# Two attention steps per round with each exponential beside one FFN group, and another order of query chunks

## The chip, the cores and the metric

The kernel runs on one NeuronCore of a Trainium2 chip. The metric is the device time of the program in microseconds (us), the median over its runs. A ratio compares the fast runs of one kernel with those of the kernel before in the same rounds, on the same chip, so it is not quite the ratio of the medians that are quoted beside it. The three later sessions ran on three chips; across sessions, compare ratios rather than medians. Profiles come from one execution each.

Engines: PE is TensorE's matmuls, PEld its weight loads, ACT is ScalarE, DVE is VectorE, POOL is GpSimd, SP is the engine that issues most transfers. The granted clock is the share of full speed at which TensorE was allowed to run; 1.00 is full speed, and 0.50 I call half clock. A tile is a buffer; PSUM is the memory that takes TensorE's products.

## The reference, cut to what matters

A causal attention with 8 batches, 8 heads, 576 tokens, 64 channels per head and 16 extra "beacon" keys that every query sees, followed by a gated feed-forward network (FFN, often called ReGLU) over the 4608 tokens of all batches:

```python
k_all = concat([beacon_k, k]); v_all = concat([beacon_v, v])
scores = where(causal, -1e9, q @ k_all.T / 8)
x = softmax(scores) @ v_all                       # (8, 8, 576, 64) -> x: (4608, 512)
out = (relu(x @ w_gate) * (x @ w_val)) @ w_out    # 512 -> 1536 -> 512
```

## The kernel before

Heads are worked on in pairs `p` (four pairs per batch). The queries of a batch are cut into three chunks: chunk 0 has 240 columns and one step (step 0), chunk 1 has 256 columns and two steps (1 and 2), chunk 2 has 80 columns and one step (step 3). I call chunks 0 and 1 long and chunk 2 short.

One step is: score matmuls (L262), exp on ScalarE (L270), masks on GpSimd (L273), then, one round later, the products of exp with the values and with ones (L293). After a chunk's last step VectorE takes the reciprocal of the row sums (L300) and multiplies it in (L302), which writes `xT`, the input of the FFN. I call these two operations the epilogue of the chunk.

FFN work comes in groups. An "up" group is 4 gate matmuls (L320), a ReLU on ScalarE (L323), 4 value matmuls (L326) and a multiply on VectorE (L328). A "down" group is 12 matmuls (L333) and a copy. Both use the same two PSUM buffers `f`. An FFN tile of 512 tokens has 12 up and 4 down groups.

```python
CHUNKS = ((0, 240, 0, 0), (240, 256, 1, 2), (496, 80, 3, 3))   # first column, columns, first and last step
...
psb = main.enter_context(tc.tile_pool(name="psb", bufs=4))       # e, the exponentials
s_ps = main.enter_context(tc.tile_pool(name="s_ps", bufs=2, space=bass.MemoryType.PSUM))
o_ps = main.enter_context(tc.tile_pool(name="o_ps", bufs=2, space=bass.MemoryType.PSUM))
f_ps = main.enter_context(tc.tile_pool(name="f_ps", bufs=2, space=bass.MemoryType.PSUM))
...
    def up(self, nf, c0, c1):
        ...
        g = f_ps.tile([P, M_TILE], FP32, name="f")
        for ki in range(KM):
            nc.tensor.matmul(g[:, :n], wg[:, ki, nf * P:(nf + 1) * P], x[:, ki], ...)      # L320
        gs = fsb.tile([P, M_TILE], FP32, name="g")
        nc.scalar.activation(gs[:, :n], g[:, :n], AF.Relu)                                 # L323
        u = f_ps.tile([P, M_TILE], FP32, name="f")
        for ki in range(KM):
            nc.tensor.matmul(u[:, :n], wv[:, ki, nf * P:(nf + 1) * P], x[:, ki], ...)      # L326
        nc.vector.tensor_mul(self.h[:, nf, c0:c1], gs[:, :n], u[:, :n])                    # L328
...
# the main loop: a round ("double step") takes two attention steps and up to two FFN groups
for s0 in range(0, len(work) + STRIDE, STRIDE):
    ...
    for s in range(s0, s0 + STRIDE):
        for act in later.pop(s, []):     # loads, casts and transposes for the next batch
            act()
        if s < len(work):
            b, p, i = work[s]
            qk(pr, i)
            softmax(pr, i)
    for g in queue[:STRIDE]:             # two FFN groups
        g()
    del queue[:STRIDE]
    for s in range(s0 - STRIDE, s0):     # value products of the round before
        ...
        av(pairs[b, p], i)
```

In each batch `work` goes through chunk 0 of the four pairs, then chunk 1, then chunk 2. The scheduler is in manual mode, so each engine runs its instructions in the order in which they are written. 32 groups (the last two FFN tiles) are left over after the loop: the tail. After 4 of those groups stands a count that checks that all row sums are in range.

## Time and profile before

| | before |
|---|---|
| median of the first two runs | 486.41 us (485.93 to 486.9) |
| profiled span | 482.4 us |
| one batch in the steady part (119.27 to 165.95) | 46.68 us, 8 double steps |
| rounds of that batch with two up groups | 5.0, 6.2, 6.3, 5.4, 5.4, 5.2 us |
| start of batch 2 / the last round with scores | 119.27 / 392.79 us |

The page of the kernel before, its first lines and two rows of the timeline in 40 slices (each digit is the busy share in tenths):

```profile
span 482.4 us, 9099 instructions
PE 394.4 (82%) x3505; PEld 204.2 (42%) x3505; DVE 239.8 (50%) x322; ACT 190.3 (39%) x290; POOL 132.0 (27%) x293
PE   0113848777989998999899989998998899799994
DMA  9999997695569257824793396439720001002002
```

TensorE is nearly full from the eleventh slice (about 120 us) on. The first quarter is different: there the transfers are busy and TensorE is not. So two stages with different limits have to be read one by one.

The waits of the kernel before (engine, tile and line that waited, who it waited for, us in total, times, longest):

```profile
POOL half L238 <- DMA raw<-in_q_dram: 71.6, 25, 13.5
PE f L320 <- ACT g L323: 16.4, 33, 1.0
PE f L326 <- ACT g L323: 9.2, 14, 0.7
PE f L320 <- DVE xT L302: 7.1, 2, 6.9
```

In the steady part nearly all of TensorE's idle is a wait for the ReLU (`g`, L323). One round shows why. This is the timeline of the kernel before, from 177.51, first TensorE (start, duration, instruction, count, then the idle time before it and what ended it):

```profile
177.51 0.56 PE L262 MATMUL s<-qT,kT 64*128 64x256 bf16 x8
178.00 1.04 PE L320 MATMUL f<-xT,wg 128*128 128x512 bf16 x4
178.87 1.03 PE L326 MATMUL f<-xT,wv 128*128 128x512 bf16 x4
180.29 1.02 PE L320 MATMUL f<-xT,wg 128*128 128x512 bf16 x4 [0.39 <-ACT g L323]
182.00 1.02 PE L326 MATMUL f<-xT,wv 128*128 128x512 bf16 x4 [0.69 <-ACT g L323]
```

ScalarE and VectorE in the same round of the same timeline:

```profile
178.03 1.73 ACT L270 ACTIVATE e<-s 128x1024 bf16<-128x1024 f32 x2 [1.43 <-PE s L262]
179.64 0.60 ACT L323 ACTIVATE g<-f 128x512 f32<-128x512 f32 x1
181.35 0.60 ACT L323 ACTIVATE g<-f 128x512 f32<-128x512 f32 x1 [1.11 <-PE f L320]
...
177.90 1.65 DVE L300 RECIPROCAL r<-o 128x240 f32<-128x240 f32 x1
179.58 0.41 DVE L302 TENSOR_TENSOR xT<-o,r 128x240 bf16<-128x240 f32 x1
179.90 1.65 DVE L300 RECIPROCAL r<-o 128x240 f32<-128x240 f32 x1
181.58 0.41 DVE L302 TENSOR_TENSOR xT<-o,r 128x240 bf16<-128x240 f32 x1
181.91 0.68 DVE L328 TENSOR_TENSOR hT<-g,f 128x512 bf16<-128x512 f32 x1
```

The gate product is complete at about 179.0, but ScalarE is still in its second exponential and starts the ReLU at 179.64. The second gate product waits for the buffer that this ReLU frees. VectorE has two long epilogues in its queue (4.0 us), so the first FFN multiply comes only at 181.91. In the built program the second value product waits for ScalarE here: it was given the buffer of the second gate product, since the first value product's buffer is still held by that multiply (which reads it until 182.59, after the second value product has started). So it waits for the second ReLU, until 181.95.

### The profile page before, as it was taken

Reading aid. Unit: us, or ns where it says so; the run is one execution under the profiler, and the core shown is the slowest. Engines: PE = TensorE matmul, PEld = TensorE weight load, DVE = VectorE, ACT = ScalarE, POOL = GpSimd, SP = SyncE. Lnnn points to the kernel's source line nnn. Section 1 sums busy time; section 2 is a strip of 40 time slices with the busy share of each in tenths; the row PEclk is TensorE's granted clock in tenths of the full one; section 3 lists DMA queues with packets and bytes.
Section 4 is the critical chain, followed back from the end, with each engine's and each line's share of the span. In section 5 each row is a group of like instructions: output and inputs, shape, how many; then the busy total and the mean of one; then the engine's idle time right before and its main releaser. Section 6 shows DMA issues by size and latency. Waiting matters only on the chain.

```text
span 482.4 us, 9099 instructions
## 1 busy us (share of the span) xinstructions
PE 394.4 (82%) x3505; PEld 204.2 (42%) x3505; DVE 239.8 (50%) x322; ACT 190.3 (39%) x290; POOL 132.0 (27%) x293
## 2 busy tenths in 40 slices
PE   0113848777989998999899989998998899799994
PEld 0012635454434544454454445544454454244442
DVE  0033525855486448636762777277528653330320
ACT  2122414444445344534443445354444442122321
POOL 2162135343424332423251335134421110000000
PEclk9998859999999999999999999999999999899998
DMA  9999997695569257824793396439720001002002
GB/s 163 191 198 194 134 198 118 136 202 105 135 108 180 72 133 139 170 72 111 164 145 108 86 175 130 118 81 192 102 89 3 1 18 73 0 1 87 1 13 80
DMA packets 166145, 53.37 MB, mean 111 GB/s; under 512 B 155728, under 2 KB 161488, under 8 KB 166096
## 3 DMA queue, kind: packets, MB, share of 16 engines
q1 hardware_dynamic: 160320, 48.01, 49.2%
q0 software_dynamic: 5776, 4.72, 7.0%
q8 instruction: 29, 0.48, 0.4%
q14 instruction: 20, 0.16, 0.1%
HBM read 38.27 MB, written 9.44 MB: 99 GB/s over the span
## 4 chain that ended last, share of the span: by engine, by line
PE 52%; DMA 13%; SPq 9%; issue 8%; ACT 8%; DVE 5%; POOL 3%; ACTq 0%; DVEq 0%; POOLq 0%
PE f L333 19%; PE f L320 11%; PE f L326 11%; PE o L293 7%; DMA raw<-in_v_dram 6%; ACT g L323 5%; SPq L220 5%; DMA raw<-in_k_dram 5%; SPq L243 4%; DVE r L300 4%; PE s L262 3%; ACT e L270 3%; DMA raw<-in_q_dram 2%; POOL e L273 1%; POOL v L238 1%
## 5 line engine op out<-in xcount | busy, mean ns | idle before, releaser
L300 DVE RECIPROCAL r<-o 128x240 f32<-128x240 f32 (+2 forms) x96 | 129.9, 1353 | 91.4 <-PE o L293 76.3
L270 ACT ACTIVATE e<-s 128x736 bf16<-128x736 f32 (+3 forms) x128 | 103.7, 861 | 104.9 <-PE s L262 103.6
L320 PE MATMUL f<-xT,wg 128*128 128x512 bf16 (+2 forms) x480 | 116.2, 364 | 25.8 <-ACT g L323 16.4
L328 DVE TENSOR_TENSOR hT<-g,f 128x512 bf16<-128x512 f32 (+2 forms) x120 | 75.9, 633 | 106.5 <-PE f L326 92.4
L326 PE MATMUL f<-xT,wv 128*128 128x512 bf16 (+2 forms) x480 | 115.4, 364 | 9.3 <-ACT g L323 9.2
L323 ACT ACTIVATE g<-f 128x512 f32<-128x512 f32 (+2 forms) x120 | 66.8, 557 | 89.8 <-PE f L320 89.8
L333 PE MATMUL f<-wo,hT 128*128 128x512 bf16 x432 | 96.2, 379 | 0.7 <-ACT g L323 0.7
L273 POOL TENSOR_SCALAR_AFFINE_SELECT e<-e 128x256 bf16<-128x256 bf16 (+2 forms) x160 | 58.8, 388 | 96.8 <-ACT e L270 96.5
L326 PEld LDWEIGHTS <-wv 128*128 128x128 bf16 x480 | 47.6, 99 | 70.1 <-issue 26.9
L320 PEld LDWEIGHTS <-wg 128*128 128x128 bf16 x480 | 43.4, 99 | 72.0 <-issue 38.0
L238 POOL CAST half<-raw 128x512 bf16<-128x512 f32 (+1 forms) x70 | 42.4, 613 | 103.8 <-DMA raw<-in_q_dram 71.6
L293 PE MATMUL o<-e,v 128*64 128x80 bf16 (+3 forms) x704 | 57.8, 238 | 9.9 <-POOL e L273 9.8
L262 PE MATMUL s<-qT,kT 64*128 64x80 bf16 (+2 forms) x704 | 36.1, 236 | 33.3 <-DMA qT<-half 25.2
L333 PEld LDWEIGHTS <-hT 128*128 128x128 bf16 x432 | 41.1, 98 | 49.9 <-issue 2.0
L293 PE MATMUL o<-e,ones 128*64 128x80 bf16 (+3 forms) x704 | 53.9, 233 | 0.0
L293 PEld LDWEIGHTS <-v 128*64 128x64 bf16 (+1 forms) x704 | 35.6, 111 | 36.1 <-issue 35.2
L336 ACT COPY ob<-f 128x512 f32<-128x512 f32 x36 | 21.1, 586 | 67.4 <-PE f L333 67.4
L238 POOL CAST v<-raw 128x512 bf16<-128x512 f32 (+1 forms) x40 | 24.5, 613 | 61.9 <-DMA raw<-in_v_dram 61.9
L262 PEld LDWEIGHTS <-kT 64*128 64x128 bf16 x704 | 21.6, 98 | 40.1 <-issue 25.8
L302 DVE TENSOR_TENSOR xT<-o,r 128x240 bf16<-128x240 f32 (+2 forms) x96 | 34.3, 357 | 3.3
L293 PEld LDWEIGHTS <-ones 128*64 128x64 bf16 (+1 forms) x704 | 34.9, 112 | 0.1
L238 DVE CAST half<-raw 128x512 bf16<-128x512 f32 (+1 forms) x5 | 2.4, 477 | 24.5 <-DMA raw<-in_k_dram 24.5
(19 smaller groups left out, 17.0 us busy)
## 6 DMA issues: line engine op xcount, KB each, us to landing
out_dram<-ob SPq DMA_DIRECT2D x36, 256.0 KB
raw<-in_q_dram SPq DMA_DIRECT2D x32, 256.0 KB
raw<-in_k_dram SPq DMA_DIRECT2D x24, 256.0 KB
raw<-in_v_dram SPq DMA_DIRECT2D x24, 256.0 KB
raw<-in_k_dram SPq DMA_DIRECT2D x8, 224.0 KB
raw<-in_v_dram SPq DMA_DIRECT2D x8, 224.0 KB
wg<-in_moe_w_gate_dram POOLq DMA_DIRECT2D x4, 384.0 KB, 6.2
wv<-in_moe_w_val_dram POOLq DMA_DIRECT2D x4, 384.0 KB, 7.3
```

The source lines that it names most:

```text
L238: copy(dst, self.raw[x, t][:n])
L262: nc.tensor.matmul(s[:, a, c:c + n], pr.batch.kT[rows, pr.p, kt * P:(kt + 1) * P], pr.batch.qT[rows, pr.p, q0:q0 + n], start=True, stop=True)
L270: nc.scalar.activation(e[:, :, :n], pr.s[i][:, :, :n], AF.Exp, scale=scale)
L273: nc.gpsimd.affine_select(out=e[:, :, c:c + m], in_=e[:, :, c:c + m], pattern=[[0, 2], [1, m]], compare_op=ALU.is_ge, fill=0.0, base=base, ...
L293: nc.tensor.matmul(o[rows, part, q0 - cq0:q0 - cq0 + n], w, e[:kr, a, c:c + n], start=(i == first and j == 0 and part == 0), stop=(i == la ...
L300: nc.vector.reciprocal(r[:, :cn], o[:, 1, :cn])
L302: nc.vector.tensor_mul(xT[:, pr.p, t0:t0 + cn], o[:, 0, :cn], r[:, :cn])
L320: nc.tensor.matmul(g[:, :n], wg[:, ki, nf * P:(nf + 1) * P], x[:, ki], start=(ki == 0), stop=(ki == KM - 1))
L323: nc.scalar.activation(gs[:, :n], g[:, :n], AF.Relu)
L326: nc.tensor.matmul(u[:, :n], wv[:, ki, nf * P:(nf + 1) * P], x[:, ki], start=(ki == 0), stop=(ki == KM - 1))
L328: nc.vector.tensor_mul(self.h[:, nf, c0:c1], gs[:, :n], u[:, :n])
L333: nc.tensor.matmul(o, self.h[:, nf, ms * P:(ms + 1) * P], wo[:, nf, :], start=(nf == 0), stop=(nf == NF - 1))
```

## The change

Two things at once, without adding or removing work:

1. Within a round both score products are issued first. Then each exponential is followed by one FFN group: exp, ReLU, exp, ReLU on ScalarE, where it was exp, exp, ReLU, ReLU.
2. From the second batch on (`b >= 1`) the order of chunks is: chunk 1 of all pairs, then chunk 0 and chunk 2 of each pair in turn, so that a long and a short epilogue meet in one round.

```diff
         for b in range(B):
-            for c, (_, _, first, last) in enumerate(CHUNKS):
-                for p in range(NP):
-                    for i in range(first, last + 1):
-                        work.append((b, p, i))
-                done = (b * S + CHUNKS[c][0] + CHUNKS[c][1])
-                ready[len(work)] = done
+            if b == 0:
+                for c, (c0, cn, first, last) in enumerate(CHUNKS):
+                    work += [(b, p, i) for p in range(NP) for i in range(first, last + 1)]
+                    ready[len(work)] = b * S + c0 + cn
+            else:
+                work += [(b, p, i) for p in range(NP) for i in (1, 2)]
+                work += [(b, p, i) for p in range(NP) for i in (0, 3)]
+                ready[len(work)] = (b + 1) * S
...
-            for s in range(s0, s0 + STRIDE):
+            now = [s for s in range(s0, s0 + STRIDE) if s < len(work)]
+            for s in now:
                 for act in later.pop(s, []):
                     act()
-                if s < len(work):
-                    b, p, i = work[s]
-                    pr = pairs.setdefault((b, p), Pair(batches[b], p))
-                    qk(pr, i)
-                    softmax(pr, i)
-            for g in queue[:STRIDE]:
-                g()
-            del queue[:STRIDE]
+                b, p, i = work[s]
+                qk(pairs.setdefault((b, p), Pair(batches[b], p)), i)
+            for j in range(STRIDE):
+                if j < len(now):
+                    b, p, i = work[now[j]]
+                    softmax(pairs[b, p], i)
+                if queue:
+                    queue.pop(0)()
```

## The prediction

> **What bounds the kernel now.** From 125 to 400 us TensorE is 82 to 100% busy in every 12 us window (table of windows), at a granted clock of 1.00. The timeline repeats one pattern of eight double steps, 46.7 us per batch (for example 165.95 to 212.64). The waits view puts 26.3 us of TensorE's idle on the ReLU. The timeline shows why: ScalarE runs exp, exp (178.03, 1.73 us together), then the first ReLU (179.64), though its gate product was ready 0.7 us earlier; the second gate product waits 0.31 to 0.39 us for that buffer. This agrees with the Trainium skill, "Perfetto Trace Analysis", Tensor Engine Instruction: ScalarE and VectorE are strictly in order. After two 240-column chunks VectorE's two reciprocals and multiplies (4.0 us, from 177.90) also hold back the first FFN multiply; there the second value product takes the gate's buffer and waits another 0.69 us. Before 120 us the kernel follows the loads: DMA share 0.8 to 1.3, GpSimd casts waiting for raw tiles.
>
> **What changes.** No work is added or removed. The built order shows the same FFN groups per double step, no starved queue, the same 32-group tail.
> 1. ScalarE runs exp, ReLU, exp, ReLU. The second exp (0.8 us) fits under the value product (0.87 us).
> 2. From batch 1 on: 4x(1,2), then 4x(0,3). VectorE's epilogue of a (0,3) pair is 1.65+0.41+0.65+0.24 = 2.9 us, against 4.0 for two long chunks and 1.8 for two short.
> 3. Cost: the batch's last double step now ends with a 240-column chunk that the next FFN tile reads at once (the built order shows a VectorE wait inside the first gate product): about 0.7 us per batch (multiply ends 1.8 us into the step, wanted at 1.15).
> 4. In batch 1 the first step needs the fourth k and q tiles, whose transposes are issued until 78.0 us, 4 us before use: 0 to 1 us lost. GpSimd takes both steps' casts before the first mask; little effect.
>
> **Sum for one steady batch**, estimated from trace durations (us): down steps 6.59+6.55 -> 6.6+6.55; FFN steps 5.01, 6.20, 6.31, 5.41, 5.41, 5.20 -> 5.8 (with cost 3), 5.1, 5.1, 5.0, 4.95, 5.25. Total 46.7 -> 44.4; over batches 2 to 7 14 us less. The ideal step keeps a 0.15 us wait of the second value product for the first multiply, as in the tail (1.01 against 0.86). Batch 1 has up to 5.6 us of such gaps, but is paced by loads: I take 2.5. Batch 0: 0.5. The tail loses about 1 (first gate product and final count wait for a later reciprocal).
>
> 486.4 - 14 - 2.5 - 0.5 + 1 = **470 us**, range 463 to 477. Faster by over 2%: 0.83; within 2%: 0.15; slower: 0.02.
>
> **What would show it right.** Waits: TensorE for ReLU from 26 us to under 8; gate product on VectorE's xT multiply 4 to 7 us. Timeline: (1,2) steps of 5.1 us instead of 5.4 to 6.3; period about 44.4. Busy time of TensorE (394), ScalarE (190), VectorE (240) about unchanged.
>
> **What would make it wrong.** Loads not keeping the shorter period, so that GpSimd's wait for raw tiles reaches the attention-value products; batch 1 waiting for transposes by several us; buffers assigned so that value products wait behind VectorE again; an xT wait much above 0.7 us, which could halve the gain.

## The result, and the profile after

The changed kernel took 470.56 us in the median of two runs (470.19 to 470.93), against 486.41. The ratio is 0.9674, with a 95% interval from 0.9621 to 0.9727. With five rounds in a later session (below) the ratio was 0.9719.

The first lines of the page after:

```profile
span 468.5 us, 9101 instructions
PE 394.7 (84%) x3505; PEld 206.8 (44%) x3505; DVE 239.8 (51%) x322; ACT 194.2 (41%) x290; POOL 132.1 (28%) x293
```

TensorE's and VectorE's busy times are unchanged. What shrank is idle time. The waits after:

```profile
PE f L320 <- DVE xT L302: 13.1, 9, 8.3
PE f L326 <- ACT g L323: 3.3, 7, 0.5
PE f L326 <- DVE hT L328: 2.7, 8, 0.4
PE f L320 <- ACT g L323: 1.1, 4, 0.3
```

TensorE's wait for the ReLU fell from 26.3 us (16.4 + 9.2 + 0.7 for the down products) to 4.4. Two waits on VectorE are new. One is for `xT` and is partly old: 8.3 us of its 13.1 are one wait at 48 us, which was 6.9 before. The other is for the FFN multiply.

A round with chunk 1, after, in the timeline: first TensorE, then ScalarE.

```profile
174.64 0.56 PE L262 MATMUL s<-qT,kT 64*128 64x256 bf16 x8
175.13 1.04 PE L320 MATMUL f<-xT,wg 128*128 128x512 bf16 x4
176.00 1.03 PE L326 MATMUL f<-xT,wv 128*128 128x512 bf16 x4
176.87 1.03 PE L320 MATMUL f<-xT,wg 128*128 128x512 bf16 x4
177.88 1.02 PE L326 MATMUL f<-xT,wv 128*128 128x512 bf16 x4
...
175.13 1.02 ACT L270 ACTIVATE e<-s 128x1024 bf16<-128x1024 f32 x1 [1.69 <-PE s L262]
176.20 0.60 ACT L323 ACTIVATE g<-f 128x512 f32<-128x512 f32 x1
176.70 0.81 ACT L270 ACTIVATE e<-s 128x768 bf16<-128x768 f32 x1
177.93 0.60 ACT L323 ACTIVATE g<-f 128x512 f32<-128x512 f32 x1 [0.43 <-PE f L320]
```

The ReLU now follows its gate product at once, and the second exponential runs while TensorE ends the value product and does most of the second gate product. No wait is left in brackets on TensorE. The round takes 5.08 us. Of it 0.15 us is still lost: the second value product starts 1.01 us after the gate product, not 0.87. (The durations of 1.03 us overlap; the distance between starts is what counts.) The exponential's length agrees with what the Trainium skill, "ScalarE: Activation LUTs", What ACT_TABLE_LOAD costs, gives for an activation with immediate operands, 186 ns plus 0.833 ns per column: by this formula an estimate of 1039 ns for 1024 columns, and 1.02 us here.

The first up round of each batch shows the new wait for `xT`, TensorE and then VectorE:

```profile
169.30 0.82 PE L320 MATMUL f<-xT,wg 128*128 128x512 bf16 x3
170.71 0.38 PE L320 MATMUL f<-xT,wg 128*128 128x512 bf16 x1 [0.59 <-DVE xT L302]
...
168.56 1.66 DVE L300 RECIPROCAL r<-o 128x240 f32<-128x240 f32 x1 [3.63 <-PE o L293]
170.25 0.41 DVE L302 TENSOR_TENSOR xT<-o,r 128x240 bf16<-128x240 f32 x1
```

The fourth gate matmul reads the columns of the pair whose epilogue has only just run.

Where the 13.9 us of span went, from the starts of rounds in both timelines:

| stage | before | after | gain |
|---|---|---|---|
| start to batch 2 | 119.27 | 117.84 | 1.4 |
| batch 2 to the last round with scores | 273.52 | 259.84 | 13.7 |
| from there to the end | 89.6 | 90.8 | -1.2 |

The first and the last row are of single executions and scatter by 1 to 2 us (see "Why the prediction was right"); the steady batches of these two profiles repeat to 0.01 us.

One steady batch takes 44.39 us (117.84 to 162.23) instead of 46.68. Its six up rounds take 5.84, 5.08, 5.08, 5.03, 4.95 and 5.32 us.

### The profile page after: what moved, and what is told of

Read it like the earlier page. It is cut to its first block, busy times and chain, and to the rows that moved or that the text cites. A ratio compares the mean times of both kernels' runs of the same rounds, so it can differ in the third digit from the quotient of the medians.

```text
span 468.5 us, 9101 instructions
## 1 busy us (share of the span) xinstructions
PE 394.7 (84%) x3505; PEld 206.8 (44%) x3505; DVE 239.8 (51%) x322; ACT 194.2 (41%) x290; POOL 132.1 (28%) x293
## 4 chain that ended last, share of the span: by engine, by line
PE 68%; DMA 9%; SPq 9%; DVE 7%; issue 4%; POOL 2%; ACT 1%; DVEq 0%; POOLq 0%; ACTq 0%
PE f L333 20%; PE f L326 19%; PE f L320 17%; PE o L293 8%; SPq L220 6%; DVE r L300 5%; PE s L262 4%; DMA raw<-in_q_dram 3%; SPq L243 2%; DMA rsum<-r 2%; DMA raw<-in_v_dram 2%; DMA qT<-half 1%; DVE hT L328 1%; DMA raw<-in_k_dram 1%; DVE xT L302 1%
## 5 line engine op out<-in xcount | busy, mean ns | idle before, releaser
L270 ACT ACTIVATE e<-s 128x736 bf16<-128x736 f32 (+3 forms) x128 | 110.1, 862 | 105.5 <-PE s L262 102.5
L320 PE MATMUL f<-xT,wg 128*128 128x512 bf16 (+2 forms) x480 | 118.2, 367 | 15.1 <-DVE xT L302 13.1
L273 POOL TENSOR_SCALAR_AFFINE_SELECT e<-e 128x256 bf16<-128x256 bf16 (+2 forms) x160 | 57.2, 385 | 86.0 <-ACT e L270 85.9
L293 PE MATMUL o<-e,v 128*64 128x80 bf16 (+4 forms) x704 | 57.7, 238 | 10.2 <-POOL e L273 10.2
L262 PE MATMUL s<-qT,kT 64*128 64x80 bf16 (+3 forms) x704 | 36.4, 237 | 33.3 <-DMA qT<-half 23.2
L293 PE MATMUL o<-e,ones 128*64 128x80 bf16 (+4 forms) x704 | 52.6, 233 | 0.0
L293 PEld LDWEIGHTS <-v 128*64 128x64 bf16 (+1 forms) x704 | 36.8, 112 | 35.6 <-issue 34.7
L262 PEld LDWEIGHTS <-kT 64*128 64x128 bf16 x704 | 22.9, 97 | 39.7 <-issue 27.9
L293 PEld LDWEIGHTS <-ones 128*64 128x64 bf16 (+1 forms) x704 | 35.4, 113 | 0.1
```

The costliest lines, as they stand in the source:

```text
L262: nc.tensor.matmul(s[:, a, c:c + n], pr.batch.kT[rows, pr.p, kt * P:(kt + 1) * P], pr.batch.qT[rows, pr.p, q0:q0 + n], start=True, stop=True)
L270: nc.scalar.activation(e[:, :, :n], pr.s[i][:, :, :n], AF.Exp, scale=scale)
L273: nc.gpsimd.affine_select(out=e[:, :, c:c + m], in_=e[:, :, c:c + m], pattern=[[0, 2], [1, m]], compare_op=ALU.is_ge, fill=0.0, base=base, ...
L293: nc.tensor.matmul(o[rows, part, q0 - cq0:q0 - cq0 + n], w, e[:kr, a, c:c + n], start=(i == first and j == 0 and part == 0), stop=(i == la ...
```

## The experiments

Ten runs, in three sessions. The theory: the late ReLU was the main loss, and the chunk order repairs what VectorE adds to it, at the price of a wait for `xT`. The rival for the cause: VectorE's two long epilogues in a row were the main loss, so the chunk order carries the gain. Each run was timed in five rounds against the kernel before.

| run | median, us | before in the same rounds | ratio (95%) | steady batch, us |
|---|---|---|---|---|
| changed kernel again | 471.05 | 484.29 | 0.9719 (0.9694 to 0.9744) | 44.39 |
| interleave only | 472.44 | 484.29 | 0.9753 (0.9728 to 0.9778) | 44.68 |
| chunk order only | 478.94 | 484.29 | 0.9892 (0.9871 to 0.9914) | 45.30 |
| batch 1 in old order | 470.74 | 484.29 | 0.9723 (0.9699 to 0.9747) | 44.39 |
| last two pairs: long long, short short | 466.67 | 485.75 | 0.9630 (0.9590 to 0.9670) | 43.67 |
| short short, long long, long long, short short | 464.73 | 485.75 | 0.9562 (0.9535 to 0.9589) | 43.27 |
| the same, count after 8 groups | 465.52 | 485.75 | 0.9576 (0.9536 to 0.9616) | 43.28 |
| the same, four buffers in the tail | 462.19 | 485.75 | 0.9511 (0.9482 to 0.9541) | 43.28 |
| half the loads of batches 1 and 2 (wrong result) | 466.08 | 485.00 | 0.9623 (0.9597 to 0.9649) | 44.39 |
| four buffers, count taken apart | 456.14 | 485.00 | 0.9404 (0.9378 to 0.9430) | 43.28 |

### The interleave alone

The changed kernel with the old construction of `work`:

```diff
-            if b == 0: ... else: ...        # new order
+            for c, (_, _, first, last) in enumerate(CHUNKS): ...   # as before
```

> Only the interleave of exponentials with FFN groups; the old order of chunks (long, long, then short). Main theory (the late ReLU costs most, so the interleave carries most of the gain): batch period 44.5 to 44.8 us, TensorE wait for ReLU under 10 us except after the two long chunks, ratio to before 0.970 to 0.975. Rival (VectorE's two long reciprocals in a row cost most, so the chunk order carries the gain): period above 46, ratio above 0.985.

Measured: 472.44 us, ratio 0.9753, period 44.68 us (162.49 to 207.17). The period (the time of one steady batch) was as the main theory expected, the ratio just outside (0.970 to 0.975). The rounds without a long pair behind them fell to 5.08 and 5.05 us. The two rounds after the long pairs fell only to 5.65 and 5.79 us, from 6.20 and 6.31. TensorE in the second of those, from the timeline of this run:

```profile
181.80 1.03 PE L320 MATMUL f<-xT,wg 128*128 128x512 bf16 x4
183.51 0.81 PE L326 MATMUL f<-xT,wv 128*128 128x512 bf16 x3 [0.69 <-ACT g L323]
```

The 0.69 us wait behind VectorE's queue is still there, the 0.37 us wait of the gate product for the late ReLU, which this round had before, is gone.

### The chunk order alone

The changed kernel with the old body of the round (exp, exp, then both groups):

```diff
-            for j in range(STRIDE):
-                if j < len(now): softmax(...)
-                if queue: queue.pop(0)()
+            # qk and softmax of both steps, then both FFN groups, as before
```

> Only the new order of chunks; ScalarE still runs exp, exp, ReLU, ReLU. Main theory: the two double steps of 6.2 and 6.3 us shrink to 5.4, but the first FFN step gains a 0.6 us wait for xT and the others keep their 0.3 us wait for ReLU: period 45.4 to 45.9, ratio 0.983 to 0.990. Rival (chunk order carries the gain): period under 45, ratio about 0.97. If the two halves were independent, the savings of both runs would add up to the whole change's 2.3 us per batch; I expect them to add up to about 3.1, since both repair the same two double steps.

Measured: 478.94 us, ratio 0.9892, inside what was expected; the period of 45.30 us is just under it (45.4 to 45.9). The 0.69 us wait is gone, the ReLU wait stays, here in one round:

```profile
186.10 1.02 PE L320 MATMUL f<-xT,wg 128*128 128x512 bf16 x4 [0.31 <-ACT g L323]
186.96 1.03 PE L326 MATMUL f<-xT,wv 128*128 128x512 bf16 x4
```

So the rival falls. The interleave alone saves 2.00 us per batch, the order alone 1.38, and both together 2.29, not 3.38 (3.1 was expected for the sum). The reason given beforehand, that both repair the same two rounds after the long pairs, covers a part only. Compared round by round, 0.36 of the missing 1.09 us lie in the two rounds at that place; the rest is spread over the other four up rounds, 0.13 to 0.24 us in each. The runs do not isolate why. On top of the interleave the order of the change is worth 0.29 us per batch. In the timed runs that is 0.3%, inside the intervals.

### The changed kernel again

> The changed kernel again, for a tight interval beside its parts: ratio 0.967 to 0.972. The profiles differ by 13.9 us (ratio 0.971), the two timed medians by 15.9 us (0.967); I expect the profiles' figure to be nearer.

Measured: 0.9719, just within the expectation, and near the profiles' 0.971. The first two runs of each kernel had shown 15.9 us of gain; five rounds show 13.2 us. Part of the close agreement of the first result with the predicted time was therefore luck in the runs.

### Batch 1 in the old order

```diff
-            if b == 0:
+            if b <= 1:
```

> The changed kernel, but batch 1 too keeps the old chunk order, so its first double step needs only the first two k and q tiles. If the 1.4 us wait at batch 1's start and the half clock after it are a real loss: 1.5 to 3 us faster than the changed kernel (466 to 469 us). If batch 1 is paced by the loads anyway: within 0.7 us of it.

Measured: 470.74 us, against 471.05 for the changed kernel in the same rounds. The wait at the start of batch 1 vanished (its first round took 3.93 us instead of 4.61), yet batch 2 started at 117.51 us against 117.84 and 120.03 in the two profiles of the changed kernel. These starts differ by no more than executions of one kernel do, but the length of batch 1 says the same: 39.35 us here, 39.04 and 38.97 with the wait. So the loss at batch 1's start is real where it stands and is made up later: something else paces this stage.

### Half the loads

```diff
             def part(p0, p1, a):
+                if b in (1, 2):      # only the first half of the heads; the casts read it twice
+                    nc.sync.dma_start(raw[p0:p1, :d_model // 2]..., a[:H // 2]...)
+                    return
```

> Wrong result on purpose: the changed kernel, but the q, k and v loads of batches 1 and 2 fetch only half their heads, and the casts read that half twice, so that every engine does the same work and only the load traffic is halved there. If loads pace batches 0 and 1 and swallowed the gain that the prediction hoped for: batch 2 starts at 108 to 114 us instead of 118 to 120, and the whole is 5 to 9 us faster than the changed kernel. If the engines' own order paces them: batch 2 starts within 1 us of before, time 470 to 472.

Measured: 466.08 us, about 5 us less than the changed kernel (4.7 by the ratios, since the sessions differ; 5 to 9 were expected), with a wrong result (relative error 0.57). Batch 2 started at 112.67 us; in the other runs with the new order it started between 117.17 and 121.88. The steady batch kept its 44.39 us. The table of windows for batch 1, first of the changed kernel, then of this run (window, its length, busy us and counts of PE, PEld, DVE, ACT and POOL, granted clock, DMA share, GB/s):

```profile
78.80:117.84 39.04, 33.54 (x413) 22.57 (x414) 22.06 (x36) 18.99 (x32) 17.57 (x40) 0.96 0.70 138
```

```profile
76.09:112.67 36.58, 32.83 (x412) 22.31 (x414) 21.96 (x35) 19.01 (x32) 17.34 (x40) 0.96 0.45 97
```

The engines do the same work in 2.5 us less, and batch 1 also starts 2.7 us sooner. TensorE's wait for masks (value products L293 on POOL e) fell from 10.2 to 6.4 us over the whole run. So the loads of batches 1 and 2 pace this stage. The path through GpSimd is read from the trace and not tested alone: its casts wait for raw tiles, and the masks stand behind the casts in its order. How much of the first two batches' gain was lost on that path is not shown: the mask waits were 9.8 us in the kernel before and 10.2 in the changed one.

### The `xT` wait taken away

```diff
-                work += [(b, p, i) for p in range(NP) for i in (0, 3)]
+                work += [(b, p, i) for p in (0, 1) for i in (0, 3)]
+                work += [(b, p, i) for i in (0, 3) for p in (2, 3)]
```

> The changed kernel with one difference: the last two pairs of a batch take both long chunks first and both short chunks last, so the chunk that the next FFN tile reads is finished one double step earlier. If the 0.59 us wait of the gate product for xT (and 1.08 us in the tail) is a real loss: that wait gone, the first FFN step 5.1 instead of 5.84 us, period 43.6 to 43.8 instead of 44.4, about 5 to 6 us faster than the changed kernel (464 to 467 us). If the wait is only the place where another limit shows: period unchanged.

Measured: 466.67 us (464.94 to 470.39), period 43.67 us. The first up round fell from 5.84 to 5.08 us, the wait of 0.59 us is gone, and so is that of 1.08 us in the tail. The loss was real. It costs 0.7 us per batch, as the prediction had put it. The tail as a whole did not get shorter (90.8 us in both profiles): after the stop for the count, described below, TensorE stayed at half clock for 6.8 us in this execution and for 3.4 us in the changed kernel's.

### Short pairs at both ends

```diff
-                work += [(b, p, i) for p in range(NP) for i in (0, 3)]
+                work += [(b, p, 3) for p in (0, 1)]
+                work += [(b, p, 0) for p in range(NP)]
+                work += [(b, p, 3) for p in (2, 3)]
```

> Order of the second half of a batch: short short, long long, long long, short short. The pairs of long chunks now fall where VectorE has a double step without FFN multiplies behind them. If the 0.35 us wait of the value product for the FFN multiply comes from VectorE's queue of two epilogues at that step: gone as well, period 43.2 to 43.5, 462 to 465 us. The balance of long and short chunks in each step, the stated intent of the change, would then not be what matters, but where the heavy pair falls.

Measured: 464.73 us, ratio 0.9562, period 43.27 us. The changed kernel's remaining wait of a value product for the FFN multiply, and the same round of this run:

```profile
198.34 1.02 PE L326 MATMUL f<-xT,wv 128*128 128x512 bf16 x4 [0.35 <-DVE hT L328]
```

```profile
197.90 1.02 PE L326 MATMUL f<-xT,wv 128*128 128x512 bf16 x4
```

This order has two rounds with two long chunks, which the change meant to avoid, and is faster. The heavy pairs' epilogues now run in rounds with down groups, where no FFN multiply stands behind them. (A wait of 0.20 us remains in the round before.) What counts is where VectorE's heavy rounds fall, not that each round is balanced.

### Two buffers each for gate and value products in the tail

```diff
-            g = f_ps.tile([P, M_TILE], FP32, name="f")
+            g = (s_ps.tile([P, 2, 512], FP32, name="s")[:, 0] if wide      # wide: only in the tail
+                 else f_ps.tile([P, M_TILE], FP32, name="f"))
```

> As short_ends, but in the tail the gate product uses a score buffer, which is free by then, so that gate and value products have two buffers each. The prediction said that the value product keeps a 0.15 us wait for the first multiply because two buffers are shared. If so, the tail's steps of 1.01 and 0.86 us become 0.87 each: 3 to 4 us faster than short_ends. If the 0.15 us has another cause: no change.

Measured: 462.19 us, 2.5 us less than the same order without it in the medians, less than the 3 to 4 expected. The two intervals of the ratios overlap, but all five runs (461.05 to 462.98) lie under all six of the other (463.34 to 465.06). It is 3.0 us less in the tail of the profiles (87.6 against 90.6). The starts of gate and value products, alternately 0.86 and 1.01 us apart before, are 0.86 us apart throughout, outside the spell of half clock after the count. So the remaining 0.15 us was the shared pair of buffers, as predicted. Within the attention rounds it was not tried: the score buffers that the tail borrows are in use there.

### The count in the tail: later, then taken apart

```diff
-            if j == 4:
+            if j == 8:
                 in_range = count_in_range()
```

> As short_ends, with the range count's product moved from after 4 to after 8 tail groups. If TensorE's 2.8 + 0.7 us stop there and the half clock after it are a loss of their own: 3.5 to 5.5 us faster than short_ends. If the tail is bound otherwise: no change.

Measured: 465.52 us against 464.73: no change, and the same wait to the hundredth (2.78 us) at the new place. Moving it proved nothing about the cause, but its trace does. VectorE, then TensorE, in this run:

```profile
402.79 0.69 DVE L328 TENSOR_TENSOR hT<-g,f 128x512 bf16<-128x512 f32 x1 [1.19 <-PE f L326]
403.40 0.44 DVE L348 TENSOR_SCALAR ge<-rsum 64x576 f32<-64x576 f32 x1
403.88 0.75 DVE L349 SCALAR_TENSOR_TENSOR ge<-rsum,ge 64x576 f32<-64x576 f32 x1
404.66 0.75 DVE L352 TENSOR_REDUCE ok<-ge 64x1 bf16<-64x576 f32 x1
...
405.46 0.16 PE L354 MATMUL o<-ones,ok 64*1 64x1 bf16 x1 [2.78 <-DVE ok L352]
406.37 1.87 PE L320 MATMUL f<-xT,wg 128*128 128x512 bf16 x4 [0.74 <-DVE cnt L356]
```

The three VectorE operations stand in order behind the newest FFN multiply, and the count's matmul stands right behind that multiply's own value product. TensorE waited for all four at both places that were tried. The four gate matmuls after the stop take 1.65 us to the next start instead of 0.87: half speed.

The last run gives the three operations and the matmul different places (after 4 and after 7 groups) and reads the count after 9; it also has the tail's buffers of the section above.

> As tail_psum, with the range count taken apart: VectorE's three operations after 4 tail groups, the product after 7, the reading of the count after 9. The late-count run kept the very same 2.8 us wait at its new place, so my theory of a late input fell; the new one is that the three operations stand behind the newest FFN multiply in VectorE's queue right before the product. If so: the 2.8 and 0.7 us waits go, and the half clock after them: 4 to 6 us faster than tail_psum, 456 to 458 us. If the wait is tied to something else: it stays at 2.8 us at the new place again, no change.

Measured: 456.14 us (454.77 to 457.58), ratio 0.9404. The count's matmul in this run's timeline (the line numbers are shifted) has no wait, and the matmuls after it run at full speed:

```profile
399.37 0.16 PE L359 MATMUL o<-ones,ok 64*1 64x1 bf16 x1
399.46 1.04 PE L321 MATMUL s<-xT,wg 128*128 128x512 bf16 x4
400.33 1.03 PE L327 MATMUL f<-xT,wv 128*128 128x512 bf16 x4
```

The tail, from the last round with scores to the end, is 81.4 us, 6.2 us less than with the count in one piece (87.6). By the ratios of the two sessions the gain is 5.2 us. The profile with the count in one piece had 6.8 us of half clock after the stop, this one none. In other executions that spell lasted 3.4 us; by an estimate (half of the difference) the gain would then be 1.7 us smaller.

The kernel with all of this, four buffers and the count taken apart on the order with short pairs at both ends, beats both kernels.

## Why the prediction was right

The time (470 against 470.56 us) and the direction were right. Point by point:

- The late ReLU as the main loss: right. The wait fell from 26.3 to 4.4 us, against "under 8". The interleave alone gave 2.00 of the 2.29 us per batch.
- The sum for a steady batch: right. Predicted up rounds 5.8, 5.1, 5.1, 5.0, 4.95, 5.25 us, measured 5.84, 5.08, 5.08, 5.03, 4.95, 5.32; period 44.4 against 44.39. It held because the rounds repeat to the hundredth of a microsecond, so each duration could be read from the trace and laid end to end. Batches 2 to 7: 14 predicted, 13.7 measured.
- Cost 3, the wait for `xT`: right. Predicted 0.7 us per batch; the wait is 0.59 us, and without it the round is 0.76 us shorter. In the waits view the whole group reads 13.1 us, not 4 to 7, since it includes a start-up wait of 8.3 us that the prediction did not set aside.
- Batches 0 and 1: mis-sized. The terms "Batch 1 ... I take 2.5" and "Batch 0: 0.5" summed to 3 us. One profile shows 1.4, the other profile of the changed kernel shows a loss of 0.8 (batch 2 at 120.03). Batch 1 alone did gain 2.1 and 2.2 us (41.18 us before, 39.04 and 38.97 after); batch 0 ended 0.7 and 3.0 us later instead of 0.5 earlier. But this stage scatters: the four runs with short pairs at both ends, which differ only in the tail, start batch 2 between 119.56 and 121.88. So a term of 1 or 2 us cannot be read from single profiles here, and what made batch 0 longer stays open. The runs showed that the loads pace the stage, though the DMA share of 0.8 to 1.3 in the prediction holds only to 84 us (from there to 120 us it is 0.57 to 0.98 in windows of 12 us). In batch 1 TensorE's waits for the ReLU fell from 7.0 to 1.9 us, and those for masks rose from 2.0 to 2.7 us.
- Cost 4, the transposes at batch 1's start: the wait was 1.2 to 1.6 us in these profiles, more than "0 to 1", and in all but one of them a spell of half clock came with it; by the end of batch 1 it made no difference.
- The tail: 1 predicted, 1.2 measured, of which 1.08 is the `xT` wait.
- ScalarE's busy time rose from 190 to 194 us, predicted "about unchanged". Two exponentials in a row overlap in the record (1.73 us for the pair), and apart they do not (1.02 + 0.81).
- The base: 486.4 us came from two runs. In the later rounds the kernel before had medians of 484.3 to 485.8. The predicted gain of 16.4 us was about 3 us too large against the 13.2 us of five rounds, most of it in the mis-sized start-up term; the predicted time was met partly because the base ran high, which is luck.

## What to carry to other kernels

An engine that works in order delays whatever stands behind a long instruction, so put the instruction that another engine needs next ahead of the one that has a whole round of slack. The Trainium skill, "Perfetto Trace Analysis", Tensor Engine Instruction, says that ScalarE, VectorE and GpSimd are strict FIFO; here the traces agree: the ReLU stood behind the exponential, the FFN multiply behind two reciprocals, the masks behind the casts and the count behind the multiply.

When two changes come together, run each alone: here they overlapped, the larger part came from the interleave, and the chunk order's stated aim (balance in every round) was not what mattered. Look for heavy pieces that can be put in rounds where nothing is waiting behind them.

A wait that keeps its length when its instruction is moved, as the count's did here, is a hint that it is tied to its neighbours in some queue and not to a late input. Read that queue, and test it.

## What the Trainium skill lacked or had wrong

- "TensorE: Matmul & The Clock Gate", Back-to-back issue gap, gives about 131 ns per matmul with 512 columns in a sustained stream of weight loads and matmuls, and says that the isolated formula (about 216 ns) over-counts there. In the tail with four buffers, groups of 4 such matmuls start 0.86 to 0.87 us apart for some 20 groups: 216 ns each, the isolated figure, which this page also gives elsewhere as measured back to back.
- The same page, What's actually happening, has the half clock after an idle window of about 3.4 us. Here shorter stops came before it. Nine profiles have a stop of 1.23 to 1.58 us before the first scores of batch 1, and in eight of them there were 3.4 us of half clock, beginning during the stop or within 2 us after it; in the ninth (1.26 us) there were none, nor in the three profiles without that stop. In the changed kernel's profile the stop of 1.40 us began at 77.4 us, TensorE had been 82% busy in the 4 us before, and the scores after it took 0.87 us instead of 0.49. Around the tail's two stops of 2.78 and 0.74 us there were 3.4 us of half clock in five profiles and 6.8 in six; in the run without these stops there were none. What decides between the cases is not shown.
- No page that I read gives the duration of VectorE's reciprocal: it took 0.65, 1.65 and 1.76 us for 80, 240 and 256 fp32 columns from PSUM, about 6.3 ns per column (1.11 us over 176 columns), against 0.69 us for a two-input multiply of 512 columns.
